# Attention with squared relu, then a mixture of depths: transposes, scores and attention in 64x64 tiles of TensorE

## The chip, the cores and the metric

The kernel runs on one core of one Trainium2 chip. The metric is the device time of one execution in microseconds; the time of a kernel is the median of its runs.

## The reference

Shapes: batch 8, 12 heads, 448 tokens, head dimension 64, so 768 features a token; the expert's hidden size is 1024 and its capacity 128 tokens a batch.

```python
scores = q @ k.T / sqrt(64)                  # per batch and head, 448 x 448
attn = maximum(scores, 0) ** 2 / 448
x = attn @ v                                 # then (batch, token, 768)

s = x @ w_gate                               # one number a token
top = the 128 tokens of the batch with the largest s
h = maximum(x[top] @ w1, 0)                  # 128 x 1024
y = h @ w2                                   # 128 x 768
out = x;  out[top] += sigmoid(s[top]) * y
```

## The kernel before

**Work items.** A pair of heads is called `t` (48 of them, six a batch); its place in the batch is `HP[t % 6]`, so two neighbours `t`, `t+1` are a pair from heads 0 to 5 and a pair from heads 6 to 11. Two neighbours together are `u`. Every step of the kernel is a small function, and the string `ORDER` writes out, by hand, the one order in which all of them are issued: each engine works through its own instructions in that order, and semaphores hold it where an operand isn't there. So nothing is rearranged behind the author's back: an instruction that has to wait holds up all that stands behind it on its engine.

**Loads.** `load_q` and `load_kv` (GpSimd's DMA queue) bring float32 from memory and leave bfloat16. `q_sb` has the tokens as 112 partitions of 4 consecutive tokens. `k_sb` and `v_sb` have them in two halves of the partitions: the lower 64 rows hold four tokens each and the upper 64 three (for heads 0 to 5; the other way round for heads 6 to 11), so the fourth group of 128 keys is half empty. The empty halves of `k_sb` are set to zero (`zero_halves`; for the later buffers on GpSimd, item `Zp`). There are three buffers each, one a batch. The first two heads of q and k come as float32 by other queues (`qf`, `kf`) and are converted by the items `Cq` and `Ck`. `W` loads the expert's two weights.

**Attention.** `T` turns q and k of one head pair into columns of tokens: TensorE multiplies with the identity, eight matmuls for q (L204, 112 rows in, 112 columns) and eight for k (L211, 128 rows in, 128 columns), all into one PSUM bank. The two heads of the pair go to partitions 0 to 63 and 64 to 127 of the output, so two tiles of 128 rows by 64 columns work side by side. `TE` (VectorE, L219) copies the bank to `qkt`. `S` (function `SC`, L233) makes the scores of one group of 128 keys for both heads: four matmuls in four tiles of 64 by 64, 448 columns each. The fourth group (`c == 3`) of two neighbours shares one call: half of its keys belong to `t`, half to `t+1`. `R` (ScalarE, L246) takes the relu of the two score banks to `r_sb`, `Q` (VectorE, L252) squares two such pieces at a time into `a_sb`. `V` (L261) multiplies with v: for a group of 128 keys one matmul for each head, 128 rows by 64 columns, 448 columns moving, summed in the bank `o_ps`; `V3` (L274) does the shared fourth group in four 64x64 tiles. `X` (L281 on ScalarE, L287 on VectorE, both lines of the helper `put`) scales `o_ps` into `xT_sb`, features in partitions and tokens in four chunks of 112.

**Back to rows.** For batches 0 to 4 `XR` transposes `xT_sb` on TensorE (tile `x_ps`, through the helper `mm` at L190, which splits every matmul in two column halves of 64) and `XRE` copies it to `x_sb`; for batches 5 to 7 `XB` does it by transposing DMAs on SyncE's queue. `ST` stores `x_sb` to the output.

**Mixture of depths** (class `Moe`, matmuls by `mm`): `g` multiplies by the gate (`sc_ps`), `bc`, `col`, `colE` bring the gate scores into rows and columns, `rk` counts for each token how many score higher, `hot` makes the selection matrix, `p` splits the scores into three bfloat16 parts, `sel` and `sE` pick index and gate, `xe`/`xeE` gather the tokens by a matmul, `h`/`hE` and `y`/`yE` are the two expert layers (tiles `h_ps`, `ye_ps`), and `ADD` adds the result to the output by an indirect DMA.

**PSUM.** Of eight banks four belong to the scores (two buffers of two banks). The other four (numbers 4 to 7) are handed to all other tiles by the numbers written in `ORDER`.

Of the kernel before, what the change touches and what calls it, by code (L numbers as in the profile page):

```python
# [19 lines left out]
def kernel(  # L20
# [29 lines left out]
    a_pool = ctx.enter_context(tc.tile_pool(name="a", bufs=7))  # L50
# [8 lines left out]
    NBUF = 3  # L59
    q_sb, k_sb, v_sb = [], [], []  # L60
    for i in range(NBUF):
        q_sb.append(const.tile([P, H, NC, Dh], BF16, name=f"q_sb{i}"))
        k_sb.append(const.tile([128, H, 4, Dh], BF16, name=f"k_sb{i}"))
        v_sb.append(const.tile([128, H, 4, Dh], BF16, name=f"v_sb{i}"))
    trash_ = const.tile([P, S], BF16, name="trash")
    NX = 2
    xT_sb = [const.tile([128, NM, 4, 128], BF16, name=f"xT_sb{i}") for i in range(NX)]

    HP = (0, 3, 1, 4, 2, 5)

    def key_slices(par):
        lo, hi = (4, 3) if par == 0 else (3, 4)
        return ((slice(0, 64), lo, slice(0, 64 * lo)), (slice(64, 128), hi, slice(64 * lo, S)))

    def zero_halves(t, eng):
        eng.memset(t[64:128, 0:6, 3, :], 0.0)
        eng.memset(t[0:64, 6:12, 3, :], 0.0)

    def load_q(b, h0, h1):
        nc.gpsimd.dma_start(
            out=q_sb[b % NBUF][:, h0:h1],
            in_=q[b, h0:h1].rearrange("h (p c) d -> p h c d", c=NC))

    def load_kv(t_sb, src, b, h0, h1):

        for rows, n, toks in key_slices(h0 // 6):
            nc.gpsimd.dma_start(  # L89
                out=t_sb[b % NBUF][rows, h0:h1, 0:n, :],  # L90
                in_=src[b, h0:h1, toks].rearrange("h (p c) d -> p h c d", c=n))


    qf = const.tile([P, 2, NC, Dh], FP32, name="qf")
    kf = const.tile([128, 2, 4, Dh], FP32, name="kf")
    wgf = const.tile([128, NM], FP32, name="wgf")
    nc.sync.dma_start(out=qf, in_=q[0, 0:2].rearrange("h (p c) d -> p h c d", c=NC))
    for (rows, n, toks), eng in zip(key_slices(0), (nc.scalar, nc.sync)):
        eng.dma_start(out=kf[rows, :, 0:n, :],
                      in_=k[0, 0:2, toks].rearrange("h (p c) d -> p h c d", c=n))  # L100
# [8 lines left out]
    load_q(0, 6, 8)  # L109
    nc.gpsimd.affine_select(out=ident, in_=ident, compare_op=ALU.not_equal, fill=1.0,  # L110
                            base=0, pattern=[[-1, 128]], channel_multiplier=1)
    load_kv(k_sb, k, 0, 6, 8)
    zero_halves(k_sb[0], nc.vector)
    load_q(0, 2, 4)
    load_kv(k_sb, k, 0, 2, 4)
    load_q(0, 8, H)
    load_kv(k_sb, k, 0, 8, H)
    load_kv(v_sb, v, 0, 0, 4)
    load_kv(v_sb, v, 0, 6, H)
    load_q(0, 4, 6)  # L120
    load_kv(k_sb, k, 0, 4, 6)
    load_kv(v_sb, v, 0, 4, 6)
    for t in xT_sb:
        nc.vector.memset(t[:, :, :, P:128], 0.0)
# [4 lines left out]
    slot_i = const.tile([P, CAP], INT32)  # L129
    slot_row = const.tile([P, CAP], BF16)  # L130
    tie_i = const.tile([P, NC, S], INT32)
    tie = const.tile([P, NC, S], BF16)
    tok_i = const.tile([P, NC, 2], INT32)
    NTK = 4
    tok = [const.tile([P, NC, 5], BF16, name=f"tok{i}") for i in range(NTK)]

    def Cq():
        nc.vector.tensor_copy(out=q_sb[0][:, 0:2], in_=qf)  # L138
        nc.vector.tensor_copy(out=k_sb[0][0:64, 0:2], in_=kf[0:64])

    def Ck():
        nc.scalar.copy(out=k_sb[0][64:128, 0:2, 0:3, :], in_=kf[64:128, :, 0:3, :])  # L142

    def Zp(i):

        if i < 2:
            zero_halves(k_sb[i + 1], nc.gpsimd)
        else:
            nc.gpsimd.iota(slot_i, pattern=[[1, CAP]], base=1, channel_multiplier=0)
            nc.gpsimd.iota(tok_i[:, :, 0], pattern=[[0, NC]], base=0, channel_multiplier=4)  # L150
            nc.gpsimd.iota(tok_i[:, :, 1], pattern=[[1, NC]], base=0, channel_multiplier=0)
            nc.gpsimd.iota(tie_i, pattern=[[-P, NC], [1, S]], base=0, channel_multiplier=-1)
# [4 lines left out]
    def Zs():  # L157
        nc.vector.tensor_copy(out=slot_row, in_=slot_i)
        for t in tok:
            nc.vector.tensor_copy(out=t[:, :, 0:2], in_=tok_i)  # L160
# [5 lines left out]
    def L(b, i):  # L166
        if i == 0:
            load_q(b, 0, H)
        elif i == 1:
            load_kv(k_sb, k, b, 0, 6)  # L170
            load_kv(k_sb, k, b, 6, H)
        else:
            load_kv(v_sb, v, b, 0, 6)
            load_kv(v_sb, v, b, 6, H)
# [17 lines left out]

    t_ps = {}

    def T(t, at):
        b, hp = t // NHP, HP[t % NHP]
        h0 = 2 * hp
        qs, ks = q_sb[b % NBUF], k_sb[b % NBUF]

        ps = bank(at, [128, 2 * S + 64], BF16, "t_ps")  # L200
        q0, k0, c0 = (0, S, S + 384) if t % 2 == 0 else (S + 64, 128, 0)
        for c in range(NC):
            for hh in range(2):
                nc.tensor.matmul(out=ps[64 * hh:64 * hh + 64, q0 + c * P:q0 + (c + 1) * P],  # L204
                                 lhsT=qs[:, h0 + hh, c, :], rhs=ident[:P, :P],
                                 is_transpose=True, start=(c == 0), stop=False,
                                 skip_group_check=True)
        for c in range(4):
            at_ = c0 if c == 3 else k0 + c * 128
            for hh in range(2):  # L210
                nc.tensor.matmul(out=ps[64 * hh:64 * hh + 64, at_:at_ + 128],  # L211
                                 lhsT=ks[:, h0 + hh, c, :], rhs=ident, is_transpose=True,
                                 start=False, stop=(c == 3), skip_group_check=True)
        t_ps[t] = ps

    def TE(t):
        sb = qt_pool.tile([128, 2 * S], BF16, name="qkt")
        x0 = 64 * (t % 2)
        nc.vector.tensor_copy(out=sb, in_=t_ps.pop(t)[:, x0:x0 + 2 * S])  # L219
        qkt[t] = sb  # L220

    def SC(t, c, at):
        ps = ps_pool.tile([128, 2, 512], FP32, name="s_ps", tag=f"bank{at}")
        s_ps[t, c] = ps
        for hh in range(2):
            rows = slice(64 * hh, 64 * hh + 64)
            for u in range(2):
                x, col = (t + u, 0 if u else S + 384) if c == 3 else \  # L230
                    (t, (64 if t % 2 else S) + c * 128 + 64 * u)
                q0 = S if x % 2 else 0
                nc.tensor.matmul(out=ps[64 * u:64 * u + 64, hh, :S],  # L233
                                 lhsT=qkt[x][rows, col:col + 64],
                                 rhs=qkt[x][rows, q0:q0 + S], start=True, stop=True,
                                 skip_group_check=True)


    def place(t, c):
        return (t - t % 2, t % 2 * 2 + c // 2, c % 2)  # L240

    def R(t, c):
        u, g, i = place(t, c)
        if (u, g) not in r_sb:
            r_sb[u, g] = r_pool.tile([128, 2, 2, S], BF16, name="r_sb")
        nc.scalar.activation(out=r_sb[u, g][:, i], in_=s_ps.pop((t, c))[:, :, :S], func=AF.Relu)  # L246

    def Q(u, g):
        n = 1 if g == 3 else 2
        r = r_sb.pop((u, g))  # L250
        a = a_pool.tile([128, 2, 2, S], BF16, name="a_sb")
        nc.vector.tensor_tensor(out=a[:, :n], in0=r[:, :n], in1=r[:, :n], op=ALU.mult)  # L252
        a_sb[u, g] = a

    def V(t, c, at=None):
        b, hp = t // NHP, HP[t % NHP]
        if t % 2 == 0 and c == 0:
            o_ps[t] = bank(at, [128, S], FP32, "o_ps")
        u, g, i = place(t, c)
        for hh in range(2):  # L260
            nc.tensor.matmul(out=o_ps[t][64 * hh:64 * hh + 64, :],  # L261
                             lhsT=v_sb[b % NBUF][:, 2 * hp + hh, c, :],
                             rhs=a_sb[u, g][:, i, hh, :], start=(t % 2 == 0 and c == 0),
                             stop=(t % 2 == 1 and c == 2), skip_group_check=True)

    def V3(u, at):

        b = u // NHP
        o_ps[u + 1] = bank(at, [128, S], FP32, "o_ps")
        for e in range(2):  # L270
            rows = slice(64 * e, 64 * e + 64)
            h0 = 2 * HP[(u + e) % NHP]
            for hh in range(2):
                nc.tensor.matmul(out=o_ps[u + e][64 * hh:64 * hh + 64, :],  # L274
                                 lhsT=v_sb[b % NBUF][rows, h0 + hh, 3, :],
                                 rhs=a_sb[u, 1][rows, 1, hh, :], start=(e == 1),
                                 stop=(e == 0), skip_group_check=True)
# [11 lines left out]
    def X(t, eng):  # L289
        b, hp = t // NHP, HP[t % NHP]  # L290
        put(eng, xT_sb[b % NX][:, hp, :, :P],
            o_ps.pop(t).rearrange("p (c n) -> p c n", c=NC), scale=o_scale)
# [8 lines left out]
    def XB(t):  # L301
        b, hp = t // NHP, HP[t % NHP]
        nc.sync.dma_start_transpose(
            out=rows_of(b)[:, :, hp * 128:(hp + 1) * 128],
            in_=xT_sb[b % NX][:, hp, :, :].rearrange("p c n -> p (c n)"))

# [286 lines left out]
```

## Time and profile before

| | |
|---|---|
| median of 3 runs | 228.59 us (227.69 to 228.86) |
| the profiled execution | 228.91 us, span 227.1 us |
| granted TensorE clock, mean | 0.971 |
| DMA packets | 51284, 36.95 MB |

The profile is of one execution. Its rows name line, engine, operation and tiles, `out<-in`; PE is TensorE's matmul, PEld its weight load, DVE VectorE, ACT ScalarE, POOL GpSimd and SP SyncE (POOLq and SPq are what they do for DMAs). A `128*64` in a matmul's row is the tile, rows by columns, and the shape behind it what moves through. The length shown for a matmul reaches from its start until its result has landed, so matmuls overlap, and the time that one takes from the next is read from start to start. "issue" as a releaser means that the engine waited for nothing that the profile can name.

### The profile page before, as it was taken

The numbers are of one execution on the slowest core, as the hardware profiler recorded it, in microseconds if no ns is written. First come the engines' busy times: TensorE is split into PE (matmuls) and PEld (weight loads), VectorE is DVE, ScalarE is ACT, GpSimd is POOL, SyncE is SP. The second block draws the span as 40 slices with busy tenths as digits, with TensorE's granted clock in tenths as the row PEclk, the third lists the DMA queues.
The fourth block names the chain that finished last, engine by engine and source line by source line (L and its number), as shares of the span: only waits on it lengthen the run. The fifth ranks groups of instructions, "written<-read, shape, count | busy, mean of one in ns | idle before, by whom it ended". The sixth has DMA issues, their size and how long they took to land.

```text
span 227.1 us, 8348 instructions
## 1 busy us (share of the span) xinstructions
PE 201.5 (89%) x3664; PEld 121.5 (53%) x3664; DVE 181.7 (80%) x378; ACT 180.0 (79%) x247; POOL 80.1 (35%) x112
## 2 busy tenths in 40 slices
PE   1887875999999999999999999999999999998730
PEld 0443363545665667466655667555377464566620
DVE  3379879778999798999788889988899989977210
ACT  3379955789899979999989999999789989963110
POOL 7999467114008640092224700552003000302120
PEclk9999999589999999999999999999999999999995
DMA  6998999999999999059999991999984729364713
GB/s 117 143 148 110 195 193 203 212 212 195 321 204 325 191 197 156 3 75 208 266 175 282 157 188 24 282 140 184 96 285 22 104 49 268 38 131 162 176 12 61
DMA packets 51284, 36.95 MB, mean 163 GB/s; under 512 B 24368, under 2 KB 48560, under 8 KB 50352
## 3 DMA queue, kind: packets, MB, share of 16 engines
q0 software_dynamic: 40144, 33.59, 86.4%
q1 hardware_dynamic: 10960, 2.69, 9.7%
q8 instruction: 29, 0.48, 0.8%
q10 hardware_dynamic: 144, 0.13, 0.2%
q14 instruction: 7, 0.06, 0.1%
HBM read 39.32 MB, written 14.16 MB: 235 GB/s over the span
## 4 chain that ended last, share of the span: by engine, by line
PE 82%; ACT 5%; DVE 5%; DMA 2%; issue 2%; POOLq 1%; SPq 0%; DVEq 0%; ACTq 0%
PE s_ps L233 20%; PE o_ps L261 13%; PE ye_ps L190 11%; PE h_ps L190 10%; PE xe_ps L190 6%; PE t_ps L204 5%; PE t_ps L211 5%; PE sc_ps L190 4%; ACT r_sb L246 4%; PE x_ps L190 3%; PE o_ps L274 2%; DMA kf<-in_k_dram 2%; DVE a_sb L252 1%; DVE qkt L219 1%; PE col_ps L346 1%
## 5 line engine op out<-in xcount | busy, mean ns | idle before, releaser
L246 ACT ACTIVATE r_sb<-s_ps 128x896 bf16<-128x896 f32 x168 | 145.5, 927 | 16.2 <-PE s_ps L233 15.5
L252 DVE TENSOR_TENSOR a_sb<-r_sb 128x1792 bf16<-128x1792 bf16 (+1 forms) x96 | 91.4, 969 | 3.9 <-ACT r_sb L246 3.6
L233 PE MATMUL s_ps<-qkt 64*64 64x448 bf16 x672 | 62.2, 382 | 6.1 <-ACT r_sb L246 3.4
L261 PE MATMUL o_ps<-a_sb,v_sb 128*64 128x448 bf16 x288 | 51.9, 367 | 0.7 <-DVE a_sb L252 0.6
L233 PEld LDWEIGHTS <-qkt 64*64 64x64 bf16 x672 | 19.6, 105 | 36.5 <-issue 30.1
L219 DVE COPY qkt<-t_ps 128x896 bf16<-128x896 bf16 x48 | 29.4, 620 | 8.9 <-PE t_ps L211 8.7
L190 PE MATMUL ye_ps<-w_sb,hT 128*64 128x384 bf16 x256 | 33.6, 332 | 0.7 <-ACT hT L281 0.7
L190 PE MATMUL h_ps<-xeT,w_sb 128*64 128x128 bf16 x768 | 29.8, 220 | 2.0 <-DVE xeT L285 0.9
L433 POOL DMA_INDIRECT out_dram<-gye,idx x8 | 14.1, 1768 | 49.1 <-ACT gye L281 48.3
L190 PEld LDWEIGHTS <-w_sb 128*64 128x64 bf16 x768 | 25.8, 110 | 7.1 <-issue 4.8
L89 POOL DMA_DIRECT2D k_sb<-in_k_dram x36 | 24.3, 749 | 10.5 <-DMA w_sb<-in_moe_w_dram 6.2
L89 POOL DMA_DIRECT2D v_sb<-in_v_dram x34 | 25.1, 956 | 7.3 <-DMA k_sb<-in_k_dram 4.7
L319 POOL DMA_DIRECT2D out_dram<-x_sb x8 | 5.2, 650 | 63.2 <-DMA x_sb<-xT_sb 31.7
L204 PE MATMUL t_ps<-ident,q_sb 112*64 112x112 bf16 x384 | 19.6, 227 | 4.6 <-DVE q_sb L138 4.2
L261 PEld LDWEIGHTS <-v_sb 128*64 128x64 bf16 x288 | 16.6, 109 | 12.9 <-issue 11.6
L287 DVE TENSOR_SCALAR xT_sb<-o_ps 128x448 bf16<-128x448 f32 x30 | 18.6, 621 | 5.2 <-PE o_ps L261 2.9
L211 PE MATMUL t_ps<-ident,k_sb 128*64 128x128 bf16 x384 | 20.7, 232 | 1.2 <-ACT k_sb L142 1.1
L204 PEld LDWEIGHTS <-q_sb 112*64 112x64 bf16 x384 | 14.9, 117 | 10.9 <-issue 5.2
L190 PEld LDWEIGHTS <-hT 128*64 128x64 bf16 x256 | 13.1, 109 | 10.6 <-issue 6.4
L190 PEld LDWEIGHTS <-x_sb 112*64 112x64 bf16 x384 | 14.7, 112 | 6.5 <-issue 4.6
L190 PE MATMUL sc_ps<-xT_sb,wg_rep 128*64 128x448 bf16 x96 | 17.5, 359 | 0.1
L211 PEld LDWEIGHTS <-k_sb 128*64 128x64 bf16 x384 | 14.8, 118 | 1.6 <-ACT k_sb L142 1.3
(162 smaller groups left out, 189.8 us busy)
## 6 DMA issues: line engine op xcount, KB each, us to landing
out_dram<-x_sb POOLq DMA_DIRECT2D x8, 1344.0 KB, 6.7
q_sb<-in_q_dram POOLq DMA_DIRECT2D x7, 672.0 KB, 12.0
w_sb<-in_moe_w_dram POOLq DMA_DIRECT2D x2, 1536.0 KB
v_sb<-in_v_dram POOLq DMA_DIRECT2D x15, 192.0 KB, 9.7
k_sb<-in_k_dram POOLq DMA_DIRECT2D x14, 192.0 KB, 7.4
v_sb<-in_v_dram POOLq DMA_DIRECT2D x15, 144.0 KB, 8.3
k_sb<-in_k_dram POOLq DMA_DIRECT2D x14, 144.0 KB, 9.7
q_sb<-in_q_dram POOLq DMA_DIRECT2D x3, 112.0 KB, 3.5
```

The source lines that it names most:

```text
L89: nc.gpsimd.dma_start(out=t_sb[b % NBUF][rows, h0:h1, 0:n, :], in_=src[b, h0:h1, toks].rearrange("h (p c) d -> p h c d", c=n))
L190: nc.tensor.matmul(out=out_[cs], lhsT=lhsT[:, cs], rhs=rhs, start=start, stop=stop, skip_group_check=True, **kw)
L204: nc.tensor.matmul(out=ps[64 * hh:64 * hh + 64, q0 + c * P:q0 + (c + 1) * P], lhsT=qs[:, h0 + hh, c, :], rhs=ident[:P, :P], is_transpose=T ...
L211: nc.tensor.matmul(out=ps[64 * hh:64 * hh + 64, at_:at_ + 128], lhsT=ks[:, h0 + hh, c, :], rhs=ident, is_transpose=True, start=False, stop ...
L219: nc.vector.tensor_copy(out=sb, in_=t_ps.pop(t)[:, x0:x0 + 2 * S])
L233: nc.tensor.matmul(out=ps[64 * u:64 * u + 64, hh, :S], lhsT=qkt[x][rows, col:col + 64], rhs=qkt[x][rows, q0:q0 + S], start=True, stop=True ...
L246: nc.scalar.activation(out=r_sb[u, g][:, i], in_=s_ps.pop((t, c))[:, :, :S], func=AF.Relu)
L252: nc.vector.tensor_tensor(out=a[:, :n], in0=r[:, :n], in1=r[:, :n], op=ALU.mult)
L261: nc.tensor.matmul(out=o_ps[t][64 * hh:64 * hh + 64, :], lhsT=v_sb[b % NBUF][:, 2 * hp + hh, c, :], rhs=a_sb[u, g][:, i, hh, :], start=(t ...
L287: nc.vector.tensor_scalar(out=out_, in0=in_, scalar1=scale, scalar2=None, op0=ALU.mult)
L319: nc.gpsimd.dma_start(out=out[b].rearrange("(p c) d -> p c d", c=NC), in_=x_rows[b][:P])
L433: nc.gpsimd.indirect_dma_start(out=out[0:self.b + 1].rearrange("b s d -> (b s) d"), out_offset=bass.IndirectOffsetOnAxis(ap=self.idx[:, :1 ...
```

## The change

All that `T`, `V` and `XR` do is cut into 64x64 tiles, so that four matmuls can stand in the array at once: two by column halves (the two heads), two by row halves (the two halves of the tokens, or of the features for `XR`).

- `T` and `V` now work on two neighbours `u`, `u+1` at once, each with a PSUM bank of its own, and have two parts, `TA`/`TB` and `VB`/`VA`. In the first part the lower 64 rows work for one of the two pairs and the upper 64 rows for the other; in the second part they change over. `XR` does the same with two chunks of tokens.
- Between the parts TensorE has to wait: the function `after` puts a no-operation on SyncE that waits for the last matmul of the first part, and makes the first matmul of the second part wait for that. There are 58 such places: 24 in `T`, 24 in `V`, 10 in `XR`.
- q is laid out as k and v were: four chunks of 128 tokens, of which the last is half empty. So q's loads are two DMAs instead of one, with 64 rows each, and the tokens in `xT_sb`, `x_sb`, `cols`, `hot` and the rest stand in four chunks of 128 instead of 112; the store is two DMAs. What is empty is left out of the matmuls or set to zero once; the zeroing of `k_sb` goes.
- `T` has 56 matmuls of 64 columns for two neighbours instead of 32 of 112 or 128; `V` has 28 of 448 columns instead of 12 of 128 rows and 4 of 64 rows; `XR` has 96 of 64 columns a batch instead of 48 of 128. The scores' matmuls, the relus, the squares and all copies keep their number and their size.
- `a_sb` has eight buffers instead of seven, `bc_` and `hot_` are two fixed buffers each, and a relu piece holds the same key group of both neighbours.
- `ORDER` is written anew: among other things the first transposes take two head pairs, the second batch's q and k are loaded ahead of the third batch's q, the weights ahead of the second batch's v, and transposes of the second batch begin before the last attention of the first. Evictions are given to ScalarE (`A`) and VectorE (`D`) anew.

```diff
+    def load(t_sb, src, b, h0, h1, par=0):
+        for rows, n, toks in halves(par):
+            nc.gpsimd.dma_start(
+                out=t_sb[b % NBUF][rows, h0:h1, 0:n, :],
+                in_=src[b, h0:h1, toks].rearrange("h (p c) d -> p h c d", c=n))
...
+    def after(what, k, i, last):
+        if k == 0:
+            if last:
+                done[what] = nc.sync.nop().ins
+                tc.add_manual_dep(done[what], i.ins.name, sync, reason=why)
+        elif what in done:
+            tc.add_manual_dep(i.ins, done.pop(what).name, sync, reason=why)
...
-    def T(t, at):
...
+    def T(u, k, at0=None, at1=None):
...
+        todo = [[], []]
+        for r in range(2):
+            e = k ^ r
+            h0 = 2 * HP[(u + e) % NHP]
+            for i in range(4 - r):
+                todo[r].append((e, qs, h0, i, 128 * i + 64 * r))
+            for i in range(3):
+                todo[r].append((e, ks, h0, i, 512 + 128 * i + 64 * r))
+            if r == e:
+                todo[r].append((e, ks, h0, 3, S))
+        for n in range(8):
+            for r in range(2):
+                if n < len(todo[r]):
+                    e, src, h0, i, col = todo[r][n]
+                    for hh in range(2):
+                        i_ = nc.tensor.matmul(
+                            out=t_ps[u + e][64 * hh:64 * hh + 64, col:col + 64],
+                            lhsT=src[HALF[r], h0 + hh, i, :], rhs=ident[HALF[r], HALF[r]],
+                            is_transpose=True, start=(k == 0 and n == 0),
+                            stop=(k == 1 and n == len(todo[r]) - 1), skip_group_check=True)
+                        after(("T", u), k, i_, n == 7 and hh == 1)
...
-    def V(t, c, at=None):
...
-    def V3(u, at):
...
+    def V(u, c, k, at0=None, at1=None):
...
+        for r in range(2):
+            e = r if k else 1 - r
             h0 = 2 * HP[(u + e) % NHP]
             for hh in range(2):
+                i_ = nc.tensor.matmul(out=o_ps[u + e][64 * hh:64 * hh + 64, :],
+                                      lhsT=v_sb[b % NBUF][HALF[r], h0 + hh, c, :],
+                                      rhs=a_sb[u, c][HALF[r], 0 if c == 3 else e, hh, :],
+                                      start=(k == 0 and c == 0), stop=(c == 3),
+                                      skip_group_check=True)
+                after(("V", u), k, i_, c == 2 and r == 1 and hh == 1)
...
-            mm(x_ps[b, c][:, m * 128:(m + 1) * 128], xT_sb[b % NX][:, m, c, :P], ident,
-               m == 0, m == NM - 1, is_transpose=True)
+            for r in range(2):
+                c = 2 * i + (k ^ r)
+                for u in range(2):
+                    col = 128 * c + 64 * u
+                    i_ = nc.tensor.matmul(
+                        out=x_ps[b, c][HALF[u], m * 128 + 64 * r:m * 128 + 64 * r + 64],
+                        lhsT=xT[HALF[r], m, col:col + 64], rhs=ident[HALF[r], HALF[r]],
+                        is_transpose=True, start=(k == 0 and m == 0),
+                        stop=(k == 1 and m == NM - 1), skip_group_check=True)
+                    after(("X", b, i), k, i_, m == NM - 1 and r == 1 and u == 1)
```

A stretch of the new order, from the second batch; numbers behind `TA`, `VB` and `S` are the item, the group and PSUM banks:

```
VB,10,0,6,4 VB,10,1 R,12,1 S,12,2,0 VB,10,2 y,0,0,5 R,12,2 Q,12,1 S,13,2,1 VA,10,0
VA,10,1 R,13,2 VA,10,2 VA,10,3 S,14,2,0 L,4,0 X,10,D y,0,0,6 X,11,A y,0,0,7 S,15,1,1
```

447 lines of the change are left out of this document (210 added, 237 removed).

## The prediction

> **What bounds the kernel now.** I read the page's busy row first, then stretches of the span, then what the weight loads wait for, then TensorE's instructions in order of time.
>
> ```profile
> span 227.1 us, 8348 instructions
> PE 201.5 (89%) x3664; PEld 121.5 (53%) x3664; DVE 181.7 (80%) x378; ACT 180.0 (79%) x247; POOL 80.1 (35%) x112
> ```
>
> ```profile
> 20.00:40.00 20.00, 15.07 (x240) 8.60 (x238) 17.45 (x37) 15.01 (x22) 12.92 (x19) 1.00 1.44 196
> 58.00:200.50 142.50, 140.92 (x2668) 85.30 (x2664) 129.72 (x267) 132.37 (x183) 41.04 (x51) 1.00 0.97 169
> 200.50:227.10 26.60, 15.10 (x334) 11.39 (x330) 8.79 (x27) 5.65 (x11) 3.72 (x3) 0.88 0.47 104
> 60.00:80.00 20.00, 19.85 (x364) 12.13 (x363) 18.39 (x40) 19.40 (x27) 9.02 (x13) 1.00 1.36 259
> ```
>
> Columns of a stretch: length, then busy time of PE, PEld, DVE, ACT and POOL (instructions in brackets), granted clock, DMA share, GB/s. From 58.0 to 200.5, the steady stage, PE is busy 140.92 of 142.50 us. ACT has 132.37 (93%) and DVE 129.72 (91%), so two others stand close behind. From 20 to 40 nothing is full: ACT 15.01 of 20. The end, 26.6 us, is one batch's chain.
>
> Not all of PE's busy time is work:
>
> ```profile
> PEld L233 <- issue: 30.1, 104, 1.1
> PEld L190 <- issue: 20.6, 78, 1.1
> PEld L261 <- issue: 11.6, 47, 0.5
> ```
>
> ```profile
> 94.96 0.38 PE L261 MATMUL o_ps<-a_sb,v_sb 128*64 128x448 bf16 x2
> 95.17 0.33 PE L190 MATMUL ye_ps<-w_sb,hT 128*64 128x384 bf16 x2
> 95.34 0.27 PE L190 MATMUL sel_ps<-tok,hot__1560 112*64 112x5 bf16 x8
> 95.46 0.36 PE L261 MATMUL o_ps<-a_sb,v_sb 128*64 128x448 bf16 x2
> 95.66 0.33 PE L190 MATMUL ye_ps<-w_sb,hT 128*64 128x384 bf16 x2
> 104.28 0.36 PE L261 MATMUL o_ps<-a_sb,v_sb 128*64 128x448 bf16 x2
> 104.57 0.57 PE L233 MATMUL s_ps<-qkt 64*64 64x448 bf16 x8
> 105.07 0.38 PE L190 MATMUL sc_ps<-xT_sb,wg_rep 128*64 128x448 bf16 x2
> ```
>
> The three wait rows count 229 stops with no engine to blame. The time rows show what they are. Two attention matmuls of 448 columns take 0.20 us from start to start when the next group has the same tile shape (95.46 to 95.66). When the next is a 64x64 group they take 0.29 (104.28 to 104.57): 0.10 more. Eight score matmuls, two groups of 0.19, take 0.50 when a 128x64 group follows: 0.12 more. So each change of tile shape stops PE for about 0.11 us. In the order of PE's instructions I count 275 changes of shape before and 197 after.
>
> **The change part by part.** *Shape changes.* 78 fewer x 0.11 = 8.6 us less on PE.
>
> *Transposes of q and k (T).*
>
> ```profile
> 33.21 0.39 PE L204 MATMUL t_ps<-ident,q_sb 112*64 112x112 bf16 x8 [0.42 <-DMA k_sb<-in_k_dram]
> 34.48 0.40 PE L204 MATMUL t_ps<-ident,q_sb 112*64 112x112 bf16 x8
> L204 PE MATMUL t_ps<-ident,q_sb 112*64 112x112 bf16 x384 | 19.6, 227 | 4.6 <-DVE q_sb L138 4.2 <-DMA k_sb<-in_k_dram 0.4
> L211 PE MATMUL t_ps<-ident,k_sb 128*64 128x128 bf16 x384 | 20.7, 232 | 1.2 <-ACT k_sb L142 1.1
> ```
>
> Three T calls of 16 matmuls take 34.48 - 33.21 = 1.27 us, 0.42 each; 48 make 20.3 us. Afterwards there are 1344 matmuls of 64 columns, laid out as 15 steps of up to four tiles for each two calls, 24 x 15 = 360 steps. No row shows four tiles at 64 columns. The nearest is sel: 8 matmuls in 95.46 - 95.34 = 0.12 us, four steps of two tiles, 0.031 a step, though only 5 columns move; there the load of 64 weight columns must be the term. I take 0.031 for a step of four: 360 x 0.031 = 11.2, so 9.1 less. Bounds: four at once at 0.031 is the low end; matmuls that come no faster than T's rows show, 0.42 / 16 = 0.026 each, is the high end, 1344 x 0.026 = 34.9, or 14.6 more.
>
> *Output transposes (XR).*
>
> ```profile
> 31.31 1.17 PE L190 MATMUL x_ps<-ident,xT_sb 128*48 128x128 bf16 x36
> 32.42 0.37 PE L346 MATMUL col_ps<-unit_f,bc__396 1*112 1x1 f32 x4
> L190 PE MATMUL x_ps<-ident,xT_sb 128*64 128x128 bf16 (+1 forms) x240 | 9.9, 220 | 0.4 <-ACT xT_sb L281 0.4
> ```
>
> 36 take 1.11 us less one shape change, 1.00: 0.056 a pair, 120 pairs, 6.7 us. After: 480 in 120 steps of four, 3.7 us by the same price; 3.0 less, with the same doubt.
>
> *Scores and attention.* The 672 score matmuls stay. Attention goes from 288 + 96 matmuls to 672, from 144 pairs and 24 fours to 168 fours of 448 columns; a group costs 0.19 to 0.20 either way. Nothing changes but the shape.
>
> *Row halves that change over.* 58 times (24 T, 24 V, 10 XR) PE now waits until the last matmul of the first half has landed and SyncE has passed that on. Everything behind it on PE, scores included, waits too, and ACT with them.
>
> ```profile
> 214.37 0.60 ACT L281 ACTIVATE hT<-h_ps 128x512 bf16<-128x512 f32 x1 [2.94 <-PE h_ps L190]
> 215.02 2.79 PE L190 MATMUL ye_ps<-w_sb,hT 128*64 128x384 bf16 x32 [0.69 <-ACT hT L281]
> L303 SPq DMA_TRANSPOSE x_sb<-xT_sb x18: 1189/1196/2138, 142.7 to 203.5; - x18
> ```
>
> One hop between engines takes 215.02 - 214.97 = 0.05 us; two hops and a little for SyncE are 0.13. With the matmul's own 0.36 (448 columns) or some 0.19 for short ones (an estimate: T's rows have 0.23 for twice the columns), the gap is 0.49 for V and 0.32 for T and XR, counted from the last start. In the written order 18 of the 58 have nothing else between the halves (about 0.32 lost beyond their own group), 5 have 0.14 us of work (0.18 lost), the rest have 0.3 to 1.9: 5.8 + 0.9 + 0.4 = 7.1 us more. Below, it could be nothing, if PE would have waited for ACT anyway. Above, SyncE also issues the 18 transposing DMAs of 1.2 us (max 2.1), and about 15 of the waits stand behind those: up to 18 us. In the order most have two relu-paced score groups between, so I take 1 us on the path.
>
> *Sum on PE:* -8.6 - 9.1 - 3.0 + 7.1 = -13.6 us, some 10 of it in the steady stage. That is more than ACT leaves: 142.50 - 132.37 = 10.1.
>
> *What is late next: ACT.*
>
> ```profile
> L281 ACT ACTIVATE xT_sb<-o_ps 128x448 bf16<-128x448 f32 x18 | 9.9, 548 | 3.0 <-PE o_ps L261 2.7 <-PE o_ps L274 0.2
> L281 ACT ACTIVATE hT<-h_ps 128x512 bf16<-128x512 f32 x14 | 8.4, 601 | 7.2 <-PE h_ps L190 6.9
> ```
>
> Its 168 relus stay. Seven xT evictions come over from DVE (7 x 0.548 = 3.8 us), six hT go to DVE (6 x 0.601 = 3.6), and two bc, with one gye and one xeT changing places: ACT's sum moves by less than 1 us, and so does DVE's. Full use of ACT would gain 10.1 us, the old 93% nothing. I take the 97% of 60 to 80 us (19.40 of 20): 132.37 / 0.97 = 136.5, **6.0 less**.
>
> *The loads of the second batch.*
>
> ```profile
> 4.00:16.00 12.00, 9.28 (x109) 5.03 (x111) 6.28 (x10) 6.63 (x8) 11.53 (x20) 1.00 1.29 156
> 16.00:20.00 4.00, 3.17 (x54) 1.50 (x50) 3.64 (x10) 3.40 (x6) 3.85 (x7) 1.00 0.38 35
> 20.00:36.00 16.00, 12.65 (x200) 7.53 (x198) 13.45 (x28) 11.46 (x17) 10.43 (x16) 1.00 1.48 193
> 16.76 0.96 POOL L82 DMA_DIRECT2D q_sb<-in_q_dram  x1
> 36.45 3.34 ACT L246 ACTIVATE r_sb<-s_ps 128x896 bf16<-128x896 f32 x4 [3.44 <-PE s_ps L233]
> q_sb<-in_q_dram POOLq DMA_DIRECT2D x7, 672.0 KB, 12.0
> ```
>
> DMA runs at 156 to 193 GB/s except from 16 to 20 us, where the next q load waited behind GpSimd's iotas and zeroing and was issued at 16.76. At 33.21 T waited for k, and ACT stood still for 3.44 us before 36.45. The new order issues the q load ahead of the iotas, has no zeroing on GpSimd, and puts the second batch's k ahead of the third batch's q: 672 KB at 193 GB/s = 3.5 us, plus about 3 us of the hole. It also puts the second batch's v behind both weight loads, which takes some back. From 0 to 6.5; I take **5.0 less**.
>
> *Small terms.* q comes in two DMAs with 64 rows instead of one, seven times, and each store in two: 13 more GpSimd issues in all, of up to 1 us (0.96 in the row at 16.76), off the path (POOL 35%). The first transposes now need heads 6 and 7 as well, whose k is issued as GpSimd's fourth and fifth load; the first relu may be 3 us later, but loads pace the first batch; I take 1.0 more (0 to 3). T now holds two of the four PSUM banks beside the scores' instead of one, from its first half to its second copy; I put nothing down for it, and what it could cost is in rival C. At the end the last two evictions and their DMAs leave together and the selection matmul stands ahead of the gather: 0.4 more (0 to 1.5).
>
> **Sum:** 227.1 - 6.0 - 5.0 + 1.0 + 1.0 + 0.4 = 218.5 us of span. The profiled execution took 228.91, 1.8 beyond its span, and lies 0.3 above the median: **220.0 us**.
>
> **The rivals.** *A: small matmuls are limited by how fast PE takes instructions (slower).* Place: T and XR, 1824 matmuls. At 0.031 for two tiles instead of four they take 28 us, what they took before; PE saves 1.5, only the start's gain stays: about 226. It decides against the change from some 0.022 us a matmul. At T's old 0.026 they take 47.4 us, 20 more than before; PE is then the bound again with 19 more, about 14 of it in the steady stage: 239. For it: nothing in the trace goes faster than sel's 0.015. Against: a group of four score matmuls takes 0.19 us, no more than two attention matmuls of the same columns (0.20), so four tiles do get their instructions side by side there. Chance 0.07 for the mild form, 0.12 for the hard one.
> The Trainium skill speaks for this rival (TensorEngine Tiling (Array Packing), Performance Considerations): every matmul has some 60 cycles of overhead, so one of 64 columns is at the floor and a dimension already small should not be divided for tiles. By that page's figure 1824 matmuls one after another would take an estimated 46 us at 2.4 GHz; sel's rows contradict it for two tiles at once, and for four no run here shows it.
>
> *B: the change-over waits stall PE (slower).* Price: 0.3 us more on each of the 58, 17 us, two thirds on the path, or SyncE busy with its DMAs for a whole 1.2 us ahead of 10 of them: 220.0 + 12 = 232. It decides from about 0.2 us more per wait. For it: PE is in order. Against: the order puts other matmuls between most halves. Chance 0.13.
>
> *C: ACT and DVE cannot be filled beyond 93%.* Three engines equally full wait for each other; the steady stage gains 0 to 1: 225 to 226, still faster by the start. Chance 0.13; with the start's gain lost too, 229: 0.05.
>
> **How the numbers follow.** My forecast has 0.50. Range 212 to 232: below, ACT at 100% (4.1 less), all of the start's 6.5 (1.5 less) and none of the three small terms (2.4 less); above, B's centre. That leaves out the hard form of A and half of B, some 0.18. A measurement of this kernel can tell about 0.5% (1.1 us) from no change. Faster: the forecast, mild A and C, 0.70, of which 0.04 goes to the two others, since mild A and C lie close to the edge: 0.66. Same: C without the start's gain, 0.05 and 0.02 of that, 0.07. Slower: hard A and B, 0.25 and 0.02, 0.27.
>
> **What would show it.** Right: PE's busy share falls to 80 to 85% with ACT above 90% from 58 us to the last relu; a T pair's 30 matmuls run in about 0.25 us; the first relu of the second batch starts before 32 us; "issue" stops of weight loads fall by some 70. Wrong: T steps of 0.06 us or more (A); PE waiting at T, V or XR for SyncE for more than 10 us in total (B); ACT still at 93% with PE idle (C).

## The result, and the profile after

The changed kernel takes **256.9 us** (median of 4; 254.2 to 258.2) against 228.7 for the kernel before, measured beside it: 1.116 times as long, 95% interval 1.107 to 1.124. Forecast were 220.0, in a range of 212 to 232. (Medians are of all runs; ratios leave out executions that were disturbed, so the two need not agree to the last digit.) The profiled execution took 254.2 us.

The busy row and the queue of instruction packets on the page after, and that queue's row on the page before (the first number is packets, then MB):

```profile
span 252.1 us, 10605 instructions
PE 196.4 (78%) x4768; PEld 122.0 (48%) x4768; DVE 187.7 (74%) x385; ACT 179.2 (71%) x246; POOL 84.8 (34%) x123
q8 instruction: 37, 0.61, 1.0%
```

```profile
q8 instruction: 29, 0.48, 0.8%
```

The shares of all three engines are lower than before (TensorE's 78% for 89%), in a longer span: nothing is full. Stretches after, from 58 us to the last relu, and from there to the end:

```profile
58.00:221.50 163.50, 143.37 (x3676) 88.40 (x3671) 138.99 (x276) 137.75 (x193) 47.78 (x63) 1.00 0.85 140
221.50:252.10 30.60, 15.34 (x264) 11.47 (x255) 8.41 (x26) 5.05 (x9) 4.42 (x4) 0.82 0.47 92
```

ACT is at 84% of the steady stage (93% before), PE at 88% (99% before), and the end takes 30.6 us instead of 26.6. TensorE in order of time, four places of the trace after:

```profile
104.97 0.31 PE L223 MATMUL t_ps<-ident,q_sb 64*64 64x64 bf16 x14
105.09 0.32 PE L223 MATMUL t_ps<-ident,k_sb 64*64 64x64 bf16 x16
105.33 0.35 PE L182 MATMUL ye_ps<-w_sb,hT 128*64 128x384 bf16 x2
...
60.88 0.38 PE L271 MATMUL o_ps<-a_sb,v_sb 64*64 64x448 bf16 x3 [1.67 <-issue]
...
143.73 0.77 PE L182 MATMUL h_ps<-xeT,w_sb 128*64 128x128 bf16 x21 [1.59 <-issue]
...
149.92 0.72 PE L271 MATMUL o_ps<-a_sb,v_sb 64*64 64x448 bf16 x9 [2.35 <-issue]
```

The first three rows say that the price of the new tiles was right: a burst of 30 transposes, eight steps, lies between 104.97 and 105.33, and 0.11 of that is the change of shape behind it: 0.03 us a step. The other rows are new. TensorE stands still for 1.6 to 2.4 us with no engine to blame, in the middle of a group (at 60.88 one of four attention matmuls had already started, 2 us earlier), and at no particular kind of work.

Counting TensorE's instructions (every weight load, matmul and other record of the trace, from 0) shows what these places share: the first matmuls after the stops are numbers 1730, 5569 and 5825, that is 194, 193 and 193 in a block of 256. In the sixteen traces of this case, after 45 us, all 73 stops of over 0.65 us without a releaser are at 193 or 194. (The expectations below leave the 32 weight loads of `col`'s float32 matmuls, four a batch, out of the count. So the place seems to slide from 192 to 170 there, and their sums of stops differ from those here by up to some 2 us.)

The instruction queue moves packets of 16384 bytes, 37 of them, against 9553 instructions of TensorE, 37.3 blocks of 256 at 64 bytes each; before, 29 against 7366, 28.8 blocks. Single packets in the trace: one from 147.60 to 148.57, TensorE goes on at 149.92; one from 141.54 to 142.52, on at 143.73; one from 58.31 to 59.41, on at 60.88. So TensorE **ran out of instructions**, and went on 1.2 to 1.5 us after the next block had landed.

All of TensorE's time, worked out from the trace: each interval between two matmuls' starts is split into streaming at the rates of the rows (0.19 us for a group of 448 columns, 0.03 for 64), up to 0.125 us for a change of shape, and the rest. Two of the experiments, described further down, stand beside: e9 with fewer instructions in the changed kernel, e12 with more in the kernel before.

| us | before | after | e9 | e12 |
|---|---|---|---|---|
| streaming, T and XR | 27.6 | 16.0 | 16.0 | 27.7 |
| streaming, all else | 130.8 | 135.5 | 131.5 | 135.4 |
| changes of shape | 28.5 | 20.0 | 19.8 | 28.6 |
| gaps under 0.25 us | 11.6 | 14.0 | 14.8 | 12.9 |
| stops over 0.25, at 193 or 194 of a block, after 50 us | 1.7 | 14.8 | 1.2 | 18.3 |
| other stops over 0.25 | 13.1 | 35.3 | 38.8 | 13.5 |
| ahead of the first matmul, behind the last | 13.8 | 16.5 | 16.0 | 13.7 |
| span | 227.1 | 252.1 | 238.0 | 250.2 |

The change took 20.1 us from TensorE (11.6 of transposes, 8.5 of shapes), nearly as forecast, and stops gave back 35.3: 13.1 at the blocks' place and 22.2 elsewhere. Not every stop of TensorE lengthens the kernel: e9 has still more of the other stops and is 14 us shorter. The other stops, by what ended them (from the waits of TensorE and of its weight loads):

```profile
PE s_ps L243 <- ACT r_sb L251: 8.2, 16, 2.1
PE t_ps L223 <- DVE q_sb L132: 7.0, 1, 7.0
PE sel_ps L182 <- DVE tok L375: 4.1, 2, 3.9
...
PE t_ps L223 <- DMA q_sb<-in_q_dram: 1.7, 1, 1.7
PE o_ps L271 <- SPq L194: 1.5, 2, 1.0
PE t_ps L223 <- SPq L194: 1.2, 4, 0.5
```

```profile
PEld L271 <- SPq L194: 4.0, 7, 1.2
PEld L223 <- SPq L194: 3.8, 12, 0.8
```

Scores wait for relus 8.2 us (3.4 before), line 194 is the change-over through SyncE, and the selection of the last batch waits 3.9 us for VectorE.

### The profile page after: what moved, and what is told of

Same layout as the page of the kernel before. It is cut to its first block, busy times and chain, and to the rows that moved or that the text cites. A ratio compares the mean times of both kernels' runs of the same rounds, so it can differ in the third digit from the quotient of the medians.

```text
span 252.1 us, 10605 instructions
## 1 busy us (share of the span) xinstructions
PE 196.4 (78%) x4768; PEld 122.0 (48%) x4768; DVE 187.7 (74%) x385; ACT 179.2 (71%) x246; POOL 84.8 (34%) x123
## 4 chain that ended last, share of the span: by engine, by line
PE 42%; ACT 20%; DVE 18%; issue 10%; POOL 3%; DMA 2%; SPq 2%; POOLq 1%; DVEq 0%; ACTq 0%
ACT r_sb L251 15%; PE s_ps L243 10%; PE o_ps L271 9%; PE h_ps L182 8%; DVE a_sb L258 7%; DVE trash L380 4%; PE t_ps L223 4%; PE ye_ps L182 3%; PE xe_ps L182 3%; PE sc_ps L182 3%; DVE qkt L232 2%; ACT xT_sb L280 2%; DMA k_sb<-in_k_dram 2%; SPq L301 2%; DVE hot_sb L387 1%
## 5 line engine op out<-in xcount | busy, mean ns | idle before, releaser
L251 ACT ACTIVATE r_sb<-s_ps 128x896 bf16<-128x896 f32 x168 | 145.7, 928 | 35.6 <-PE s_ps L243 34.1
L271 PE MATMUL o_ps<-a_sb,v_sb 64*64 64x448 bf16 x672 | 48.4, 369 | 8.9 <-issue 6.6
L243 PEld LDWEIGHTS <-qkt 64*64 64x64 bf16 x672 | 24.7, 109 | 33.5 <-issue 23.6
L232 DVE COPY qkt<-t_ps 128x896 bf16<-128x896 bf16 x48 | 28.4, 617 | 10.4 <-PE t_ps L223 10.3
L271 PEld LDWEIGHTS <-v_sb 64*64 64x64 bf16 x672 | 20.3, 110 | 24.2 <-issue 12.4
L82 POOL DMA_DIRECT2D k_sb<-in_k_dram x34 | 22.5, 684 | 26.7 <-DMA w_sb<-in_moe_w_dram 13.8
L448 POOL DMA_INDIRECT out_dram<-gye,idx x8 | 13.7, 1706 | 48.3 <-ACT gye L280 40.1
L182 PE MATMUL ye_ps<-w_sb,hT 128*64 128x384 bf16 x256 | 27.5, 332 | 0.7 <-ACT hT L280 0.7
L223 PE MATMUL t_ps<-ident,q_sb 64*64 64x64 bf16 x672 | 16.0, 202 | 12.5 <-DVE q_sb L132 7.0
L223 PEld LDWEIGHTS <-q_sb 64*64 64x64 bf16 x672 | 13.2, 112 | 19.5 <-DVE q_sb L132 7.0
L380 DVE SCALAR_TENSOR_TENSOR trash<-bc_sb,cols,tie 128x448 bf16<-128x448 f32 (+1 forms) x32 | 21.7, 677 | 0.5
L182 PE MATMUL xe_ps<-hot_sb,x_sb 128*64 128x128 bf16 x384 | 16.6, 244 | 2.2 <-issue 1.4
L182 PEld LDWEIGHTS <-hT 128*64 128x64 bf16 x256 | 12.8, 109 | 9.3 <-issue 4.3
L82 POOL DMA_DIRECT2D q_sb<-in_q_dram x20 | 16.1, 895 | 2.9 <-DVE hot_sb L387 1.3
L280 ACT ACTIVATE xT_sb<-o_ps 128x448 bf16<-128x448 f32 x25 | 13.5, 548 | 4.8 <-PE o_ps L271 4.5
```

The lines of the kernel that those rows point to most:

```text
L82: nc.gpsimd.dma_start(out=t_sb[b % NBUF][rows, h0:h1, 0:n, :], in_=src[b, h0:h1, toks].rearrange("h (p c) d -> p h c d", c=n))
L182: nc.tensor.matmul(out=out_[cs], lhsT=lhsT[:, cs], rhs=rhs, start=start, stop=stop, skip_group_check=True, **kw)
L223: i_ = nc.tensor.matmul(out=t_ps[u + e][64 * hh:64 * hh + 64, col:col + 64], lhsT=src[HALF[r], h0 + hh, i, :], rhs=ident[HALF[r], HALF[r]] ...
L232: nc.vector.tensor_copy(out=sb, in_=t_ps.pop(t))
L243: nc.tensor.matmul(out=ps[64 * u:64 * u + 64, hh, :S], lhsT=sb[rows, col:col + 64], rhs=sb[rows, :S], start=True, stop=True, skip_group_ch ...
L251: nc.scalar.activation(out=r_sb[u, c][:, t % 2], in_=s_ps.pop((t, c))[:, :, :S], func=AF.Relu)
```

## The experiments

The theories: **fetch** (blocks of 256 instructions are used up faster than they come), **change-over** (the waits through SyncE), **order** (the new order of steps and loads costs the time, whatever the tiles).

**e1: T, XR and V in 128-row tiles again, in the new order.**

```diff
-    lhsT=src[HALF[r], h0 + hh, i, :], rhs=ident[HALF[r], HALF[r]]     # T
+    lhsT=src[p, h0 + hh, i, :], rhs=ident[p, p]    # p: rows 0:128, of the last chunk 64
+    mm(x_ps[b, c][:, m * 128:(m + 1) * 128], xT[:, m, 128 * c:128 * c + 128], ident, ...)
+    lhsT=v_sb[:, h0 + hh, c, :], rhs=a_sb[u, c][:, k, hh, :]
```

> The changed kernel with its order, loads and layout, but T, XR and V (but for the half chunk) in 128-row tiles again: 7337 instructions on TensorE instead of 9523, no change-over wait in V and XR, and T's two 64-row steps at its ends with six 128-row steps between them. Fetch theory (TensorE runs out of fetched instructions: stops without a semaphore, 16.0 us in the changed kernel, 1.9 before, each at the same place of a block of 256 instructions): the stops fall to under 4 us, TensorE streams about 12 us more (T 9.1, XR 3.0) and changes shape 75 to 80 times more at 0.11 us (8.6): 245 us (240 to 250). Change-over theory (the 58 waits through SyncE and what stands behind them cost 10 us): about 255. Order theory (the new order of steps and loads is what costs, whatever the tiles): 256 or more. At 232 or less the tiles alone would be to blame for everything.

Measured: **261.0 us**, 1.142 times before (1.135 to 1.149). Stops at the block's place: 1.1 us, as the fetch theory has it. But the time did not fall. The expectation was wrong in one count: in the new order these tiles change shape 370 times, not 275, 38.7 us against 20.0. With 10.3 us more of transposes, that outweighs the 13.7 us of stops and the change-overs that went. So the new order is bad for the old tiles; whether it is bad for the new ones, this run can't tell.

**e2: T alone in 128-row tiles; e3: V alone.** The same edits, one at a time.

> The changed kernel with T alone in 128-row tiles again: 8386 instructions on TensorE, of T 66 a pair of heads' couple instead of 112, in twice the streaming time (+9 us) and with some 70 more shape changes (+8 us). Fetch theory: the bursts that empty the fetched block are gone, stops fall from 16.0 to about 5 us, and the time stays near or falls a little: 252 us (247 to 257). Change-over theory: T's 24 waits are hidden behind six steps, 3 to 4 us gained against 17 us more on TensorE, of which two thirds show: 264 (260 to 268). Order theory: as the latter, 264.

> The changed kernel with V alone in 128-row tiles for its three full chunks: its 24 change-over waits are gone (the trace has 4.0 us before V for SyncE), 8954 instructions on TensorE, the same streaming time, about 90 more shape changes (+10 us on TensorE, of which some half shows). Fetch theory: stops from 16.0 to 11 to 14 us, time 257 (253 to 261). Change-over theory: 10 us or more come back before the shape changes, time 251 or less. Order theory: 259 or more.

Measured: e2 **254.0** (ratio 1.104 to 1.117), stops at the place 4.1 us; e3 **255.4** (1.105 to 1.127), stops 12.2. Both as the fetch theory had it, and neither as the others: against e2 the four-tile transposes save 7.6 us of streaming and 9.9 of shape changes, and bring 10.7 of stops; V's change-over waits are worth no more than the shape changes that replace them.

**e4, e5, e6: 128, 64 and 192 instructions more, before anything starts.**

```diff
+        ps = ps_pool.tile([128, 2, 512], FP32, name="pad_ps", tag="banks1")
+        for i in range(64):                              # e5: 32, e6: 96
+            nc.tensor.matmul(out=ps[0:64, 0, 0:64], lhsT=pad, rhs=pad, start=True, stop=True, ...)
```

> The changed kernel with 64 idle matmuls (64x64, written to a bank that is not used yet) ahead of the first transposes, while TensorE waits for the first load: 128 instructions, no work after 7 us changed. Fetch theory: the stops leave the places of the order at which they stood (61, 67, 89, 123, 144, 150, 197 us) and stand again at positions 170 to 192 of a block of 256, that is 128 instructions earlier or later in the order; their sum stays within 9 to 22 us, and the time moves with the sum (250 to 262). All other theories: the stops stand where they stood in the order, and the time is that of the changed kernel, 257 within 1%.

> The changed kernel with 32 idle matmuls (64 instructions) ahead of the first transposes; nothing else differs. Fetch theory: the stops without a semaphore stand again at positions 170 to 192 of a block of 256, 64 instructions later in the program's count, so at other steps of the order; the time follows their sum at about 0.8 us a us, by the two kernels measured so far (13.9 us of stops and 256.9; 19.0 and 260.9). Order theory (the new order sets the time, the stops are hidden behind it): 257 within 1%, whatever the sum.

> The same with 96 idle matmuls (192 instructions). Fetch theory: as before, by its own sum of stops; a sum of 8 us would give 252, one of 20 would give 262. Order theory: 257 within 1%.

Two of e4's stops, where the changed kernel stopped in V (60.88) and in h (143.73):

```profile
59.78 0.92 PE L182 MATMUL h_ps<-xeT,w_sb 128*64 128x128 bf16 x26 [1.73 <-issue]
...
141.22 0.57 PE L271 MATMUL o_ps<-a_sb,v_sb 64*64 64x448 bf16 x7 [2.00 <-issue]
```

They are instructions 1729 and 5569, place 193 of their blocks again, the same numbers in TensorE's stream, and 64 matmuls earlier in the order: now h stops, and V. The stops belong to the count of instructions and not to the work; no wait on a semaphore could move so. Sums at the place: 13.5 (e6), 14.8 (unshifted), 16.5 (e5), 19.6 us (e4); times 255.8, 256.9, 261.7, 260.9; ratios 1.115, 1.116, 1.143, 1.126 (each within 0.013). More stops, more time, though not in step.

**e7: the second couple of pairs transposed later.**

```diff
-    ... R,1,0 TA,2,7,6 Zw,D R,1,1 TB,2 S,0,3,1 TE,3 R,0,3 S,0,0,0 TE,2 L,1,0 R,0,0 S,0,1,1 Q,0,3 R,0,1 Zp
+    ... R,1,0 Zw,D R,1,1 S,0,3,1 R,0,3 S,0,0,0 L,1,0 R,0,0 S,0,1,1 Q,0,3 R,0,1 TA,2,7,6 TB,2 TE,3 TE,2 Zp
```

> The changed kernel with the second couple of pairs' transposes (TA,2 TB,2 and their evictions) moved behind the seventh score block, so that TensorE isn't held at 9.8 to 13.9 us by loads that have not landed. If the late start is carried to the end: the first eight relus 2 to 3 us sooner and the time 254. If it is absorbed by the loads of the second batch (the 24th relu was only 0.4 us later than in the kernel before): no change at the 24th relu, 257.

Measured: **258.4**, no gain. But the relus say more: the ninth starts at 18.2 us (20.4 in the changed kernel, 17.5 before), the 73rd at 98.9 (102.8 and 93.5), so the 2.2 us of the start were still there, and more; the 81st at 112.7 (113.6). In between instructions ran out:

```profile
103.92 0.37 PE L243 MATMUL s_ps<-qkt 64*64 64x448 bf16 x1 [1.86 <-issue]
```

```profile
100.00:104.00 4.00, 2.14 (x68) 1.17 (x56) 3.25 (x9) 2.32 (x3) 1.09 (x2) 1.00 0.91 184
104.00:108.00 4.00, 4.00 (x59) 2.12 (x63) 3.28 (x10) 1.90 (x3) 0.43 (x1) 0.63 0.68 252
```

The second fence is two stretches: behind the stop the granted clock is 0.63 for 4 us, so this stop cost more than its length. e7's stops at the place sum to 19.5 us.

**e8: in the kernel before, the weights loaded ahead of the second batch's v.**

```diff
-    L,1,2 T,6,7 ... T,8,7 TE,7 W,0 TE,8 ... TE,10 W,1 R,7,1
+    W,0 W,1 L,1,2 T,6,7 ... T,8,7 TE,7 TE,8 ... TE,10 R,7,1
```

> The kernel before with the two weight loads moved ahead of the second batch's v, as the changed order has them, and nothing else. If that place of the weights is what costs the new order its time between 39 and 66 us: 4 to 8 us slower, 233 to 237. If not: within 1 us, 229 to 230.

Measured: **237.7**, 1.039 (1.031 to 1.046): 8.4 us, by one wait:

```profile
PE o_ps L261 <- DMA v_sb<-in_v_dram: 7.6, 1, 7.6
```

**e10: in the changed kernel, v ahead of the weights again**, with h of batch 0 behind the attention of pairs 6 to 9.

> The changed kernel with the second batch's v loaded ahead of the two weights, and h of batch 0 moved behind VB,8 VA,8, so that it doesn't wait for its weights. Order theory (the weights ahead of v cost 8.4 us in the kernel before, 4 to 8 of them here): the 40th relu 3 to 6 us sooner, time 251 (249 to 254). If the new order has other work in place of the late v: no change, 257 within 1%. Fetch theory alone: the stops move to other steps, within 3 us either way.

Measured: **256.4**, no change. The place of the weights costs 8.4 us in the old order and nothing that this edit finds in the new one, which has other steps where the late v would be awaited. Its stops at the place sum to 9.9 us, 4.9 less than in the changed kernel, and the time did not follow; two of them were followed by 3.4 us at half the clock (from 97.2 and from 144.9 us).

**e9: matmuls of 128 weight columns in the expert part.**

```diff
-        for cs in (slice(0, 64), slice(64, lhsT.shape[1])):
-            nc.tensor.matmul(out=out_[cs], lhsT=lhsT[:, cs], rhs=rhs, start=start, stop=stop, ...)
+        nc.tensor.matmul(out=out_, lhsT=lhsT, rhs=rhs, start=start, stop=stop, ...)
```

> The changed kernel with the matmuls of the expert layers, gate, gather and selection (h, y, xe, sc, sel), which are written as two halves of 64 weight columns, each as one matmul of 128: 7955 instructions on TensorE instead of 9523, order, attention and transposes untouched. Fetch theory: blocks last longer, stops of over 0.25 us at positions 165 to 195 after 50 us fall from 16.5 us to 6 to 9, and the time to 249 (245 to 253), if one matmul of 128 columns streams like the two halves beside each other (0.056 us a step of h, 0.16 of y). Order theory: 257 within 1%.

Measured: **241.2 us** (238.9 to 242.7), 15.7 less than the changed kernel by the medians, with no step moved. The kernel before took 224.2 to 230.4 beside it (median 228.8), too wide for a ratio of e9, e10 or e11.

```profile
PE 192.8 (81%) x3984; PEld 115.8 (49%) x3984; DVE 186.5 (78%) x385; ACT 179.2 (75%) x246; POOL 85.0 (36%) x123
q8 instruction: 31, 0.51, 0.8%
```

```profile
58.00:209.00 151.00, 141.61 (x3101) 84.75 (x3102) 138.73 (x276) 138.71 (x193) 47.74 (x64) 1.00 0.92 151
```

31 packets instead of 37, stops at the place 1.2 us instead of 14.8, the last relu at 209.1 instead of 221.5, ACT at 92% of the steady stage.

**e12, e13: the same dose on the kernel before.** e12 splits each matmul of h and xe into two of 64 moving columns; e13 is e9's edit.

```diff
+        parts = (slice(0, 64), slice(64, 128)) if n == 128 and not kw else (None,)   # e12
```

> The kernel before with each matmul of h and xe as two with 64 moving columns instead of one with 128: 9640 instructions on TensorE instead of 7336 (the changed kernel has 9523), order, loads and tiles untouched; at 0.031 us a step instead of 0.056 this adds 576 x 0.006 = 3.5 us of streaming. Fetch theory: stops at the place of the block appear in the kernel before as well, 8 to 15 us where it has 1.7, time 238 to 248. Without fetch stops: 229 to 233.

> The kernel before with its two halves of 64 weight columns as one matmul of 128, as in the run that took 15.7 us from the changed kernel: 5528 instructions on TensorE. If those 15.7 us were fetch stops: the kernel before has 1.7 us of them to lose, and its matmuls of 128 columns stand beside 128x64 tiles of T and V, between which a shape change may cost up to 0.11 us: 229 to 240, not faster than 227. If a matmul of 128 columns is cheaper by itself: 5 us or more faster, under 224.

e12: **253.0**, 1.106 (1.097 to 1.114). With as many instructions as the changed kernel, and nothing else of it, the kernel before becomes as slow:

```profile
span 250.2 us, 10652 instructions
...
PEclk9999997799999999999799999999999999999995
...
q8 instruction: 37, 0.61, 1.0%
```

```profile
65.08 0.51 PE L193 MATMUL h_ps<-xeT,w_sb 128*64 128x64 bf16 x21 [2.37 <-issue]
...
121.80 0.38 PE L238 MATMUL s_ps<-qkt 64*64 64x448 bf16 x3 [3.00 <-issue]
```

The table's last column adds it up: 16.6 us of new stops at the place, 4.6 more of other streaming, 1.3 of small gaps, 0.4 of other stops. The clock's row has a 7 in the slice from 119 to 125 us, where the stop of 3.00 lies; the kernel before has a 9 there. The time is 5 us over the upper expectation.

e13: **246.2**, 1.076 (1.070 to 1.082), above both expectations. No stop at the place is left, and it is slower: gaps under 0.25 us go from 11.6 to 30.7, since matmuls of 128 columns now stand beside tiles of 64: 446 changes of shape instead of 274, and the new ones, between 128x64 and 128x128, cost 0.10 to 0.12 us each as the others do, 172 x 0.11 = 19. A matmul of 128 columns isn't cheaper by itself (a step of h takes 0.057 us in e9 and e13, 0.056 as two halves), and what e9 gained came from the stops, 13.6 of 14.1 us of span: in the changed kernel every other tile is 64x64, and the edit adds no change of shape (189, and 196 without it).

**e11 and e14: what the runs point to, together.** e11 is e9 with XR in 64x128 tiles, e7's and e10's moves and the last selection behind the gather; e14 is e9 with e7's move alone.

> The changed kernel with everything together that the runs point to: matmuls of 128 columns in the expert part, XR in two 64x128 tiles (half its instructions, same streaming), the second couple's transposes behind the seventh score block, v ahead of the weights, and in the last batch the selection behind the gather: 7475 instructions on TensorE. If the causes add (stops -10 to -12, start -2 to -3, loads -4, tail -1): 239 (234 to 245), still over the kernel before. If the order alone set the time: 249 to 252.

> The changed kernel with matmuls of 128 columns in the expert part and the second couple's transposes moved behind the seventh score block. With the fetch stops gone, the 4 us that the moved transposes gained up to the 72nd relu are no longer given back: 238 (236 to 240) against 241.2. If the start is absorbed by the loads: 241.

e11: **243.0**, within its range and yet 1.8 over e9: v first and the later selection brought nothing (its 73rd relu is 2.6 us later than e9's). e14: **238.7**, 1.046 (1.040 to 1.052), 2.5 under e9: with the stops gone, the start is carried (73rd relu at 95.4, e9's at 97.5; last at 207.5). By the ratios, 1.116 and 1.046, e9's edit and the start gained 16 us together. It is the best version of the changed kernel that was found, and 10 us over the kernel before. No version that beats both was found.

## Why the prediction was wrong

The forecast took 8.6 us from the span; 25.0 were added: 8.1 up to the 41st relu (63.9 us, 55.9 before), 12.8 from there to the last relu (157.5, 144.7), 4.0 behind it (30.6, 26.6). In e9, nearly without stops at the blocks, the three are 7.1, 1.4 and 2.2. So the stops made most of what the middle lost, and not what was lost ahead of it.

*What bounds the kernel; shapes; T; XR:* right. Shape changes: 8.5 us less (8.6 forecast), T 8.9 (9.1), XR 2.7 (3.0). The prediction weighed the 60 cycles for each matmul of the Trainium skill (TensorEngine Tiling (Array Packing), Performance Considerations) against sel's rows: the trace after has 30 matmuls in eight steps of 0.03 us, 0.008 each, so as a price per matmul the rule does not hold for four tiles.

*The rivals:* this is the step that failed first. A asked whether small matmuls are limited "by how fast PE takes instructions", and priced it per matmul, at T and XR; what the next block of instructions costs all the other work stood nowhere in the sum, which is to say at nothing. The limit lies in how long 256 instructions last. Over the sixteen kernels here, after 45 us, 68 blocks were used up in less than 4.5 us, and 38 of them ended in a stop of over 0.25 us, 0.9 us on the mean of all 68; of 218 that lasted over 6 us, 19 did, 0.1 on the mean. A burst of T's 112 instructions in 0.5 us, where two pairs took 64 in 0.85 before, shortens a block by itself. The profile before showed it, unquoted: two stops without a semaphore, each at place 193 of its block, 1.7 us together from start to start, whose idle time is in these rows of TensorE's waits:

```profile
PE h_ps L190 <- issue: 0.9, 1, 0.9
PE s_ps L233 <- issue: 0.4, 1, 0.4
```

30% more instructions, and the order's bursts, made 14.8 us of them. e9 takes 13.6 us of stops away and 15.7 of time (14.1 of the span); e12 adds 16.6 and takes 24.4 more time. (In A's mild form T and XR take 28 us against 27.0 before, so TensorE saves 0.2 us there, not 1.5.)

The Trainium skill (Runtime: NRT & Kernel Launch, Instruction fetch mechanics) states that instructions are fetched in blocks of 16 KiB, 256 instructions, by the engine's own queue, and that this is mostly hidden because the engine issues more slowly than the blocks arrive. The trace agrees with the blocks and not with hidden: 14.8 us.

*Change-over waits:* +7.1 forecast; the gaps that end on SyncE's semaphore sum to 6.7 us, the longest 1.2. Right; what they cost in time was not tried alone.

*What is late next (ACT at 97%, -6.0):* wrong, the second step that failed, and only in part as a consequence. ACT is at 84%, waiting 34.1 us for scores (15.5 before). Without the stops it is at 92% (e9), hardly what it was, waits 24.3 us for scores, and goes from the 41st relu to the last in 146.1 us (144.7 before): 20 us less work on TensorE gained the steady stage nothing. Rival C had the better number there; which wait holds ACT in e9 the runs do not show.

*Loads of the second batch (-5.0):* the term was mis-sized. The first relu of that batch starts at 35.5 us, not before 32; before it was 36.4. The edge was lost by the 41st relu, 8.1 later. All of that was lost behind the 25th (39.2 us, 38.9 before); up to the 41st ACT waits 7.1 us for scores (2.3 before), and TensorE stops once at a block's place (1.7) and twice for relus (3.1, at 46.73 and 48.33, behind copies of `x_sb` on ACT). The weights ahead of v, set at part of 0 to 6.5, cost 8.4 where they alone are moved (e8), and nothing by e10. The start is 2 us of it (e7: 41st relu 1.8 sooner; e14 against e9: the same). Which steps of the new order cost the rest stays open.

*Small terms:* first relus +1.0 forecast; the first is 1.9 us late, the 17th 4.7, as the second couple waits for its loads. The end +0.4 forecast, 4.0 measured, of which 3.9 is the selection behind VectorE; moving it (e11) gained nothing that shows; there the gather waits for `hot` instead, 2.8 us in two.

*The signs that were named:* T's burst in 0.25 us and some 77 fewer issue stops of weight loads came true. They spoke of the tiles, and the tiles were right. PE's share of 80 to 85% with ACT above 90%, and the relu before 32 us, did not come (78%, 84%, 35.5); of the signs of being wrong none came either (T steps 0.03 us, 6.7 us for SyncE, ACT below 93%). None of them looked at stops without a releaser by their place.

## What to carry to other kernels

Count an engine's instructions, not only its busy time: where 256 of them are used up in less than about 4.5 us (38 of 68 such blocks stopped here, 54 of 167 that lasted 4.5 to 6), look for stops without a releaser at one place of the block, and expect them to grow with every edit that cuts work into smaller pieces. Smaller tiles that are cheaper each can be paid for by making other matmuls larger, if they bring no new change of shape. And a gain early in the kernel is worth only what the stops behind it leave.

## What the runs showed of the hardware that was not expected

TensorE's stops at the end of a block last up to 3.0 us, and from 45 us on the place is the same, 193 or 194, in every trace that has them (e13 has none). Of the 106 stops of over 0.25 us at that place, 103 end 1.2 to 1.7 us after the block's packet has landed. In none of 513 blocks does TensorE pass the place less than 1.16 us after the landing. The packet itself begins only about when TensorE passes the same place one block earlier (-0.1 to 4.3 us after it, 5th to 95th percentile): the lead is one block. What delays it goes with the other DMA traffic: after 20 us, where the DMA engines' share over the 3 us behind that passing was under 0.94, the packet began 0.8 us after it on the median, and where it was over 1.47, 3.6 us. No experiment varied the loads for this alone, so that they are the cause is not shown.

A stop of 1.9 us was followed by 4 us at a granted clock of 0.63 (e7). In the sixteen traces, between 60 and 215 us, eleven stretches have half the clock (3.4 us each, once 6.8), and all begin during a stop of over 1.7 us or within 2.3 us behind it; most such stops are followed by none. And 64 idle instructions at the start moved the time by some 5 us (e5 against the unshifted kernel) with the work unchanged: two versions of a dense kernel can differ by 2% by the place of their blocks alone.
